# A planned attention and two-FFN kernel: twelve plan settings instead of one, another cut of d_ff, and one more engine choice

## Chip, cores and metric

The kernel runs on one core of one Trainium2 chip. The metric is the device time of one execution in microseconds; of several runs the median is given. Engines are called by their trace names where rows show them: PE is TensorE, DVE is VectorE, ACT is ScalarE, SP is SyncE, which issues the DMAs.

## The reference

Three stages follow each other. First, attention with a window and sinks (2 batches, 8 heads, 768 positions, 64 per head); then two feed-forward layers on 1536 tokens with d_model 512 and d_ff 2048, the first with a leaky activation per column (alpha), the second with softplus.

```python
keep   = (pos_k < n_sink) | ((rel >= 0) & (rel < window))   # n_sink 4, window 128
scores = where(keep, q @ k.T / sqrt(64), -1e9)
a      = exp(scores - max); a = a / (sum(a) + 1e-9); x = a @ v
h = x @ w_in1;  g = maximum(h, 0) + alpha * minimum(h, 0);       x = g @ w_out1
h = x @ w_in2;  g = maximum(h, 0) + log1p(exp(-abs(h)));         out = g @ w_out2
```

## The kernel before

Tokens are worked in four tiles (0 to 3) of 384, d_ff in 16 slices (c) of 128. An operand of a large matmul is kept as two halves: a rounded first part and the remainder (`copy`, L196, and `minus`, L205). A product is three matmuls: first by first, and the two mixed ones. For a tile and a slice, `g1` (L308) makes h with 12 matmuls into bank 4 or 5, by turns; `act1` (L328) or `act2` (L339) turns h into g and its halves on ScalarE and VectorE; `g2` (L361, layer 1) adds g's share to banks 0 to 3 with 12 matmuls; `g2_out` (L403, layer 2) does so with 9 wider ones into three banks per tile. `act2` is Abs, Exp, 1 + u (`more`, L346), Ln on the way of log1p, and three VectorE operations that put the parts together. The one at L357 is the last to read h's bank.

Weights come in eight bytes an element, and `convert` (L265) makes the two halves of one slice's weights out of them: five passes on VectorE (L291, L293, L295, L298, L206) and two on ScalarE (L282, L198). There are 16 weight buffers. Layer 2's slice c goes into the buffer of layer 1's slice c, so its load (L278) can only be issued when the last tile of layer 1 has used that slice. Attention's first loads lie in some of the same buffers.

Attention goes in 24 groups, six for each tile (`front`, L489: scores, minimum and exponential, scaling; `back`, L544: transposes, bank copies, values, halves of x).

Layer 1's order is a list of (tile, slice) at L647, made from `cuts` (L646). Tiles 0 and 1 are cut at 4 slices: tile 0 slices 0 to 3, tile 1 slices 0 to 3, tile 0 slices 4 to 15, tile 1 slices 4 to 15. Tiles 2 and 3 are cut at 8 in the same way. At the end of each run `keep_y` (L375) takes the sums out of banks 0 to 3: the first time as a copy, the second time as an add onto it (L387). For tile 3, the sum shares its memory with layer 2's step buffers of the odd slices. `split_y` (L391) makes the halves of x for layer 2 from a finished sum. Layer 2's first two tiles are cut at 8.

The order on the engines comes from a planner that runs while the program is built (`Planned`, L48). Every operation is added with a cost for each engine that may do it, the keys that it reads and writes, and a due time. `forward` (L85) is a list scheduler: at each moment a free engine takes the ready operation with the earliest due time. Where an operation may go to two engines, it is left to the other if that one would be done with it sooner, and in that comparison a queue counts: 1.8 times the cost of the ready operations on an engine that are due up to 10 us later than this one (L101 to L104). `backward` (L147) reckons from a plan how late each operation may start; `run` (L178) makes one plan from the due times written out, 12 more each from the latest starts of the one before, takes the plan with the earliest planned end, and issues the instructions in its order.

Of the kernel before, what the change touches and what calls it, by code (L numbers as in the profile page):

```python
# [34 lines left out]
class InOrder:  # L35
# [8 lines left out]
    def run(self):  # L44
        pass


class Planned:  # L48
# [33 lines left out]
            return 0.0 if a == "PE" else 0.13  # L82
        return self.AFTER[a] + (0.09 if b == "PE" else 0.0)

    def forward(self, due):  # L85

        ops = self.ops
        left = [len(o[2]) for o in ops]
        free = dict.fromkeys(self.ENGINES, 0.0)
        waiting = {e: [] for e in self.ENGINES}  # L90
        ready = {e: [] for e in self.ENGINES}
        end, on, start = {}, {}, {}

        def at(n, e):
            return max((end[b] + self.lag(on[b], e) for b in ops[n][2]), default=0.0)

        def offer(n):
            for e in ops[n][1]:
                heapq.heappush(waiting[e], (at(n, e), n))

        def queue(e, n):  # L101

            return 1.8 * sum(ops[m][1][e] for d, m in ready[e]
                             if m not in start and m != n and d <= due[n] + 10 and len(ops[m][1]) == 1)  # L104

        def elsewhere(n, e, t):
            mine = t + ops[n][1][e] + queue(e, n) - 1e-9
            return any(max(t, free[o], at(n, o)) + c + queue(o, n) < mine for o, c in ops[n][1].items() if o != e)

        for n in range(len(ops)):  # L110
            if not left[n]:
                offer(n)
        t, force = 0.0, False
        while len(start) < len(ops):
            for e in self.ENGINES:
                while waiting[e] and waiting[e][0][0] <= t + 1e-9:
                    n = heapq.heappop(waiting[e])[1]
                    if n not in start:
                        heapq.heappush(ready[e], (due[n], n))
            for e in self.ENGINES:  # L120
                if free[e] > t + 1e-9:
                    continue
                later = []
                while ready[e]:
                    d, n = heapq.heappop(ready[e])
                    if n in start:
                        continue
                    if not force and elsewhere(n, e, t):
                        later.append((d, n))
                        continue  # L130
                    start[n], end[n], on[n] = t, t + ops[n][1][e], e
                    free[e] = end[n]
                    for m in self.after[n]:
                        left[m] -= 1
                        if not left[m]:
                            offer(m)
                    break
                for x in later:
                    heapq.heappush(ready[e], x)
            nxt = [free[e] for e in self.ENGINES if free[e] > t + 1e-9]  # L140
            nxt += [waiting[e][0][0] for e in self.ENGINES if waiting[e] and waiting[e][0][0] > t + 1e-9]
            if len(start) < len(ops):
                force = not nxt
                t = min(nxt, default=t)
        return max(end.values()), start, end, on
# [32 lines left out]
    def run(self):  # L178

        self.after = [[] for _ in self.ops]  # L180
        for n, o in enumerate(self.ops):
            for b in o[2]:
                self.after[b].append(n)
        plans = [self.forward([o[3] for o in self.ops])]
        for _ in range(self.AGAIN):
            plans.append(self.forward(self.backward(*plans[-1][2:])))
        last, start, end, on = min(plans, key=lambda p: p[0])
        for n in sorted(start, key=lambda n: (start[n], n)):
            self.ops[n][0](self.nc, on[n])
# [67 lines left out]
class Ffn:  # L257
# [81 lines left out]
    def act2(self, p, due, fresh):  # L339

        add, mem, n = self.p.add, self.mem, p % 2
        h, kh = mem.bank[4 + n][:, 0:TT], ("bank", 4 + n)
        ku, kw, kl = [("step", n, i) for i in range(3)]
        (u, w, l), before = mem.step[n][0][:3], mem.step[n][1] if fresh else []

        def more(nc, e):  # L346
            if e == "ACT":
                nc.scalar.activation(w, u, AF.Copy, bias=1.0)
            else:
                nc.vector.tensor_scalar(w, u, 1.0, None, ALU.add)  # L350

        add(lambda nc, e: nc.scalar.activation(u, h, AF.Abs), {"ACT": 0.39}, [kh], [ku] + before, due)  # L352
        add(lambda nc, e: nc.scalar.activation(u, u, AF.Exp, scale=-1.0), {"ACT": 0.43}, [], [ku], due)  # L353
        add(more, {"DVE": 0.27}, [ku], [kw], due)
        add(lambda nc, e: nc.scalar.activation(l, w, AF.Ln), {"ACT": 0.43}, [kw], [kl], due)  # L355
        add(lambda nc, e: nc.vector.scalar_tensor_tensor(u, w, 1.0, u, ALU.subtract, ALU.subtract), {"DVE": 0.47}, [kw], [ku], due)  # L356
        add(lambda nc, e: nc.vector.scalar_tensor_tensor(l, h, 0.0, l, ALU.max, ALU.add), {"DVE": 0.47}, [kh], [kl], due)  # L357
        add(lambda nc, e: minus(nc, e, l, l, u), {"DVE": 0.47}, [ku], [kl], due)
        self.halves(lambda: l, kl, p, due)
# [279 lines left out]
def fast_path(tc, mem, masks, val, kqv, alpha, weights, out, loaded):  # L639


    nc = tc.nc
    plan = Planned(nc)
    ffn = Ffn(mem, plan, weights, out)
    att = Window(mem, plan, kqv)
    cuts = ((0, 4, 16), (0, 8, 16))  # L646
    layer1 = [(2 * n + t, c, a, b) for n in range(2) for a, b in zip(cuts[n], cuts[n][1:]) for t in range(2) for c in range(a, b)]  # L647
    layer2 = [(t, c) for c0 in (0, 8) for t in range(2) for c in range(c0, c0 + 8)] + [(t, c) for t in (2, 3) for c in range(16)]
    slots = 4 * [8.0] + 4 * [5.0] + 32 * [5.3] + 88 * [4.2]
    begin = [27.0]  # L650
    for s in slots:
        begin.append(begin[-1] + s)

    def at(p):

        n = max(0, min(int(p), 127))
        return begin[n] + (p - n) * slots[n]

    def groups(t):
        wanted = [8 + 3.2 * (r + 1) if t == 0 else 30 + 4 * r if t == 1 else at((0, 0, 10, 25)[t] + (0, 0.7, 2.5, 2.4)[t] * r + 0.5) for r in range(6)]  # L660
        behind = 1 if t == 1 else 0
        for r in range(6 + behind):
            if r < 6:
                G, a = 6 * t + r, wanted[r]
                if G >= loaded:
                    att.load(G, a - 20)
                att.front(G, a - 6, a - 4)
            if r >= behind:
                att.back(6 * t + r - behind, wanted[r - behind] - 2)

    plan.add(lambda nc, e: masks.first(nc, val), {"DVE": 0.9}, [("ring", 2)], [("mask", 0)], -20.0)
    for i in (1, 2):
        plan.add(lambda nc, e, i=i: masks.later(nc, i), {"DVE": 0.4}, [("ring", 2), ("mask", 0)], [("mask", i)], 5.0 * i)
    groups(0)
    groups(1)
    plan.add(lambda nc, e: nc.sync.dma_start(out=mem.alpha, in_=alpha), {"SP": 0.5}, [], [("alpha",)], 10.0)
    plan.add(lambda nc, e: nc.vector.tensor_scalar(mem.alpha, mem.alpha, -1.0, None, ALU.mult), {"DVE": 0.08}, [], [("alpha",)], 20.0)
    for c in range(16):
        d = at([p for p, x in enumerate(layer1) if x[:2] == (0, c)][0]) - 9
        ffn.convert(0, c, c, d, d - 3)  # L680
    for p, (t, c, a, b) in enumerate(layer1):
        d = at(p)
        ffn.g1(t % 3, c, p, d - 5)
        ffn.act1(c, p, d - 2)
        ffn.g2(c, p, d + 1, (c == a, c == b - 1))
        if c == b - 1:
            ffn.keep_y(t, d + 2, 4 if t == 3 and a else t, t if a else None)
        if p in (0, 23):
            groups(2 + (p == 23))
        if p == 31:  # L690
            ffn.split_y(0, 1, at(44))
        if p == 55:
            ffn.split_y(1, 2, at(58))
        if t == 3:
            w = at(42 + 2 * c if c < 8 else 64 + 2.5 * (c - 8))
            ffn.convert(1, c, c, w, w - 6)
    for p, (t, c) in enumerate(layer2):
        d = at(64 + p)
        ffn.g1((t + 1) % 3, c, p, d - 8)
        ffn.act2(p, d - 5, p < 2)  # L700
        ffn.g2_out(t, c, p, d + 1)
        if p in (0, 23):
            ffn.split_y(2 + (p == 23), p // 23, d + 10)
        if c == 15:
            ffn.store(t, d + 2)
    plan.run()
# [203 lines left out]
```

## Time and profile before

| | us |
|---|---|
| median of three runs | 636.86 (636.72 to 638.86) |
| profiled execution, its time | 637.52 |
| profiled execution, its span | 635.7 |
| PE busy | 615.2 |
| DVE busy | 478.5 |
| ACT busy | 328.9 |

The span runs from the first to the last instruction; the execution's own time is 1.8 us longer. The granted TensorE clock has a mean of 0.997 of full speed. PE's busy time is that of pipelined matmuls whose ends are modelled, so the spacing of their starts in the chain of waits is the better measure of its pace.

### The profile page before, as it was taken

The numbers are of one execution on the slowest core, as the hardware profiler recorded it, in microseconds if no ns is written. First come the engines' busy times: TensorE is split into PE (matmuls) and PEld (weight loads), VectorE is DVE, ScalarE is ACT, GpSimd is POOL, SyncE is SP. The second block draws the span as 40 slices with busy tenths as digits, with TensorE's granted clock in tenths as the row PEclk, the third lists the DMA queues.
The fourth block names the chain that finished last, engine by engine and source line by source line (L and its number), as shares of the span: only waits on it lengthen the run. The fifth ranks groups of instructions, "written<-read, shape, count | busy, mean of one in ns | idle before, by whom it ended". The sixth has DMA issues, their size and how long they took to land.

```text
span 635.7 us, 10814 instructions
## 1 busy us (share of the span) xinstructions
PE 615.2 (97%) x4192; PEld 572.1 (90%) x4192; DVE 478.5 (75%) x1119; ACT 328.9 (52%) x739; POOL 2.5 (0%) x18
## 2 busy tenths in 40 slices
PE   5789999999999999999999989999999999999996
PEld 4678999999999999999999979999999999999995
DVE  7999999955345644499966999867876777677774
ACT  4999687644533654356534765433443433343332
POOL 1000000000000000000000000000000000000000
PEclk9999999999999999999999999999999999999998
DMA  8999701121211110176007610000010100000001
GB/s 319 357 385 410 268 1 52 51 77 51 85 51 68 52 51 2 67 249 215 1 1 265 219 46 1 1 1 1 0 51 0 51 1 1 1 25 26 2 0 56
DMA packets 15035, 56.55 MB, mean 89 GB/s; under 512 B 1920, under 2 KB 4480, under 8 KB 14976
## 3 DMA queue, kind: packets, MB, share of 16 engines
q1 hardware_dynamic: 14976, 55.78, 24.5%
q8 instruction: 35, 0.57, 0.4%
q14 instruction: 24, 0.20, 0.1%
HBM read 52.63 MB, written 3.15 MB: 88 GB/s over the span
## 4 chain that ended last, share of the span: by engine, by line
PE 90%; DVE 4%; ACT 3%; issue 1%; DMA 1%; SPq 0%; ACTq 0%; DVEq 0%
PE bank L317 40%; PE bank L411 21%; PE bank L370 19%; PE bank L574 3%; PE bank L516 3%; PE bank L553 2%; PE bank L554 2%; DVE temp L298 1%; DMA temp<-kqv 1%; ACT early L527 1%; DVE g L206 0%; DVE w L206 0%; DVE r L335 0%; ACT temp L282 0%; ACT late L527 0%
## 5 line engine op out<-in xcount | busy, mean ns | idle before, releaser
L317 PE MATMUL bank<-x,w 128*128 128x384 f32 x1536 | 294.5, 337 | 2.8 <-DVE late L357 2.8
L317 PEld LDWEIGHTS bank<-x,w 128*128 128x128 f32 x1536 | 269.2, 188 | 9.7 <-DVE late L357 3.2
L370 PE MATMUL bank<-g,w 128*128 128x384 f32 x768 | 149.3, 338 | 0.0
L411 PE MATMUL bank<-w,g 128*128 128x512 f32 x576 | 143.1, 393 | 0.0
L370 PEld LDWEIGHTS bank<-g,w 128*128 128x128 f32 x768 | 133.3, 188 | 1.4
L411 PEld LDWEIGHTS bank<-w,g 128*128 128x128 f32 x576 | 107.1, 188 | 19.6
L352 ACT ACTIVATE late<-bank 128x384 f32<-128x384 f32 x64 | 31.4, 491 | 113.3 <-PE bank L317 113.3
L335 DVE SCALAR_TENSOR_TENSOR r<-r,alpha,r 128x384 f32<-128x384 f32 x64 | 39.3, 614 | 45.1 <-ACT r L334 44.8
L333 ACT ACTIVATE r<-bank 128x384 f32<-128x384 f32 x64 | 31.3, 490 | 61.7 <-PE bank L317 59.9
L350 DVE TENSOR_SCALAR late<-late 128x384 f32<-128x384 f32 x64 | 22.9, 358 | 44.0 <-ACT late L353 44.0
L355 ACT ACTIVATE late<-late 128x384 f32<-128x384 f32 x64 | 33.7, 526 | 26.1 <-DVE late L350 26.0
L527 ACT ACTIVATE late<-late,st 128x200 f32<-128x200 f32 (+1 forms) x72 | 31.8, 445 | 25.0 <-DVE st L524 25.0
L206 DVE TENSOR_TENSOR g<-late,g 128x384 fp32r<-128x384 f32 x64 | 35.6, 557 | 6.1 <-DVE g L202 0.9
L298 DVE SCALAR_TENSOR_TENSOR temp<-w,temp 128x1024 int32<-128x1024 int32 x32 | 38.8, 1215 | 1.5 <-ACT temp L282 1.5
L206 DVE TENSOR_TENSOR w<-temp,w 128x1024 fp32r<-128x1024 f32 x32 | 39.0, 1218 | 0.1
L198 ACT ACTIVATE w<-temp 128x1024 fp32r<-128x1024 f32 x32 | 34.0, 1064 | 8.1 <-DVE temp L298 8.1
L356 DVE SCALAR_TENSOR_TENSOR late<-late 128x384 f32<-128x384 f32 x64 | 35.6, 557 | 1.9
L206 DVE TENSOR_TENSOR late<-late 128x384 f32<-128x384 f32 x64 | 35.5, 557 | 1.8
L206 DVE TENSOR_TENSOR g<-r,g 128x384 fp32r<-128x384 f32 x64 | 35.5, 555 | 1.6 <-ACT g L198 0.4
L357 DVE SCALAR_TENSOR_TENSOR late<-bank,late 128x384 f32<-128x384 f32 x64 | 35.5, 556 | 0.1
L198 ACT ACTIVATE late<-bank 128x512 f32<-128x512 f32 (+2 forms) x49 | 24.8, 543 | 19.7 <-PE bank L554 14.4
L353 ACT ACTIVATE late<-late 128x384 f32<-128x384 f32 x64 | 33.6, 525 | 1.9
(98 smaller groups left out, 524.6 us busy)
## 6 DMA issues: line engine op xcount, KB each, us to landing
w<-w SPq DMA_DIRECT2D x32, 1023.8 KB, 5.8
w<-kqv SPq DMA_DIRECT2D x20, 388.0 KB, 7.3
late<-kqv SPq DMA_DIRECT2D x20, 388.0 KB, 3.5
out<-late SPq DMA_DIRECT2D x18, 128.0 KB, 1.7
spare<-kqv SPq DMA_DIRECT2D x5, 388.0 KB, 4.5
temp<-kqv SPq DMA_DIRECT2D x3, 388.0 KB, 4.4
out<-early SPq DMA_DIRECT2D x2, 256.0 KB, 3.0
out<-early SPq DMA_DIRECT2D x2, 128.0 KB, 3.9
```

Source lines behind the costliest of these rows:

```text
L198: nc.scalar.activation(out, src, AF.Copy)
L206: engine(nc, e).tensor_tensor(out, a, b, ALU.subtract)
L298: add(lambda nc, e: nc.vector.scalar_tensor_tensor(b, raw[0].rearrange("p n w -> p (n w)").bitcast(I32)[:, 0:2048:2], 13, b, ALU.logical_s ...
L317: nc.tensor.matmul(out=h, lhsT=w[:, a, kk], rhs=xt[:, b, kk], start=(kk == 0 and n == 0), stop=(kk == 3 and n == 2))
L335: add(lambda nc, e: nc.vector.scalar_tensor_tensor(n, n, mem.alpha[:, c:c + 1], r, ALU.mult, ALU.add), {"DVE": 0.54}, [("r", 0), ("alpha", ...
L353: add(lambda nc, e: nc.scalar.activation(u, u, AF.Exp, scale=-1.0), {"ACT": 0.43}, [], [ku], due)
L355: add(lambda nc, e: nc.scalar.activation(l, w, AF.Ln), {"ACT": 0.43}, [kw], [kl], due)
L356: add(lambda nc, e: nc.vector.scalar_tensor_tensor(u, w, 1.0, u, ALU.subtract, ALU.subtract), {"DVE": 0.47}, [kw], [ku], due)
L357: add(lambda nc, e: nc.vector.scalar_tensor_tensor(l, h, 0.0, l, ALU.max, ALU.add), {"DVE": 0.47}, [kh], [kl], due)
L370: nc.tensor.matmul(out=self.mem.bank[m][:, 0:TT], lhsT=w[:, a, m], rhs=g[:, b], start=(ends[0] and part == 0 and n == 0), stop=(ends[1] an ...
L411: nc.tensor.matmul(out=self.mem.bank[bk], lhsT=g[:, a, m * 128:(m + 1) * 128], rhs=w[:, b], start=(c == 0 and part == 0 and n == 0), stop= ...
L527: add(lambda nc, e, u=u: nc.scalar.activation(s[:, u, c0:], s[:, u, c0:], AF.Exp, bias=st[:, 0, u:u + 1], scale=-1.0, accum_out=st[:, 1, u ...
```

## The change

Three things are changed. `forward` takes two numbers, `ahead` and `crowd`, in place of the fixed 10 and 1.8, and `run` makes its 13 plans for each of the twelve pairs of 10, 30, 60 and 0.6, 1.0, 1.4, 1.8, then takes the plan with the earliest planned end of all. Tiles 2 and 3 are cut at 10 slices in place of 8; the halves of tile 1's result are added to the plan after tile 2's last slice, as before, which is now position 57 in place of 55. And 1 + u of `act2` may go to ScalarE, at a planner's cost of 0.43 us, beside VectorE at 0.27.

```diff
-    def forward(self, due):
+    def forward(self, due, ahead=10, crowd=1.8):
...
-            return 1.8 * sum(ops[m][1][e] for d, m in ready[e]
-                             if m not in start and m != n and d <= due[n] + 10 and len(ops[m][1]) == 1)
+            return crowd * sum(ops[m][1][e] for d, m in ready[e]
+                             if m not in start and m != n and d <= due[n] + ahead and len(ops[m][1]) == 1)
...
-        plans = [self.forward([o[3] for o in self.ops])]
-        for _ in range(self.AGAIN):
-            plans.append(self.forward(self.backward(*plans[-1][2:])))
+        plans = []
+        for ahead in (10, 30, 60):
+            for crowd in (0.6, 1.0, 1.4, 1.8):
+                plans.append(self.forward([o[3] for o in self.ops], ahead, crowd))
+                for _ in range(self.AGAIN):
+                    plans.append(self.forward(self.backward(*plans[-1][2:]), ahead, crowd))
...
-        add(more, {"DVE": 0.27}, [ku], [kw], due)
+        add(more, {"DVE": 0.27, "ACT": 0.43}, [ku], [kw], due)
...
-    cuts = ((0, 4, 16), (0, 8, 16))
+    cuts = ((0, 4, 16), (0, 10, 16))
...
-        if p == 55:
+        if t == 2 and c == 15:
             ffn.split_y(1, 2, at(58))
```

## Rows read from the trace of the kernel before

**Rows 1.** The page's busy times: engine, us busy, share, instructions.
```profile
PE 615.2 (97%) x4192; PEld 572.1 (90%) x4192; DVE 478.5 (75%) x1119; ACT 328.9 (52%) x739; POOL 2.5 (0%) x18
```

**Rows 2.** Chain of waits in order of time, full stream: start us, us, what.
```profile
326.14 2.08 PE bank L370 x12
...
332.21 2.08 PE bank L317 x12
...
548.66 2.08 PE bank L411 x9
550.74 2.10 PE bank L317 x12
```

**Rows 3.** PE's waits: line, whom it waited for, us in total, times, longest.
```profile
PE bank L516 <- DMA temp<-kqv: 5.6, 1, 5.6
PE bank L317 <- DVE late L357: 2.8, 1, 2.8
PE bank L516 <- DVE x L206: 2.1, 3, 1.1
PE bank L516 <- DVE st L531: 1.5, 1, 1.5
PE bank L574 <- ACT late L198: 1.4, 3, 0.7
PE bank L553 <- ACT early L539: 1.0, 2, 0.6
PE bank L574 <- ACT early L198: 0.5, 1, 0.5
```

**Rows 4.** Chain of waits, where the stream of PE begins.
```profile
37.64 2.02 PE bank L574 x32
39.66 2.85 PE bank L317 x15
```

**Rows 5.** Chain of waits at the change from layer 1 to layer 2.
```profile
367.64 1.14 DVE w L206
...
369.98 0.48 DVE late L357
...
370.50 2.87 PE bank L317 x15
```

**Rows 6.** Busy us by stretch; after POOL: PEclk, DMA share, GB/s.
```profile
20.00:40.00 20.00, 15.11 (x252) 11.85 (x251) 20.00 (x72) 20.00 (x63) 0.00 (x0) 1.00 0.96 364
40.00:60.00 20.00, 20.00 (x221) 17.95 (x220) 20.00 (x65) 18.73 (x51) 0.31 (x1) 1.00 1.00 400
318.00:338.00 20.00, 20.00 (x117) 20.00 (x117) 11.62 (x24) 6.18 (x14) 0.00 (x0) 1.00 0.12 41
348.00:395.00 47.00, 44.23 (x234) 41.25 (x234) 47.00 (x86) 31.88 (x54) 0.00 (x0) 1.00 0.28 99
```

**Rows 7.** Groups by line: engine, operation, shapes, count, busy us, mean ns.
```profile
L335 DVE SCALAR_TENSOR_TENSOR r<-r,alpha,r 128x384 f32<-128x384 f32 x64 | 39.3, 614 | 45.1 <-ACT r L334 44.8
L206 DVE TENSOR_TENSOR w<-temp,w 128x1024 fp32r<-128x1024 f32 x32 | 39.0, 1218 | 0.1
L298 DVE SCALAR_TENSOR_TENSOR temp<-w,temp 128x1024 int32<-128x1024 int32 x32 | 38.8, 1215 | 1.5 <-ACT temp L282 1.5
...
L353 ACT ACTIVATE late<-late 128x384 f32<-128x384 f32 x64 | 33.6, 525 | 1.9
L350 DVE TENSOR_SCALAR late<-late 128x384 f32<-128x384 f32 x64 | 22.9, 358 | 44.0 <-ACT late L353 44.0
...
L291 DVE TENSOR_SCALAR temp<-w 128x1024 bf16<-128x1024 bf16 x16 | 11.0, 689 | 0.2 <-DMA w<-w 0.2
L295 DVE TENSOR_TENSOR temp<-temp 128x1024 int16<-128x1024 int16 x16 | 11.0, 685 | 0.1
L293 DVE TENSOR_SCALAR temp<-temp 128x1024 int16<-128x1024 int16 x16 | 6.7, 420 | 0.0
```

## The prediction

> **What bounds the kernel now.** I read the page's busy times first, then TensorE's waits, then the chain of waits in order of time, and last the busy time by stretch. The busy times give TensorE 615.2 us of a 635.7 us span [rows 1]. Busy matmuls are modelled, so I checked them against the chain: in layer 2 a slice of d_ff is 12 matmuls in 2.10 us and 9 in 2.08 us, one group after the other without a gap, and in layer 1 twelve take 2.08 us [rows 2]. A slice is then 4.16 us in layer 1 and 4.18 us in layer 2, and 64 of each are 266 + 268 = 534 us. The diff leaves out or adds no matmul. So TensorE's stream can't get shorter; only its waits can. The list of them has 14.9 us in all [rows 3]: 5.6 us for the first kqv transfer, 2.8 us in one piece for VectorE's L357, and 2.1 + 1.5 + 1.4 + 1.0 + 0.5 = 6.5 us in attention. In the chain TensorE runs from 37.64 us on [rows 4], and the 2.8 us are the gap before the group that starts at 370.50 us [rows 5]. Both places are the same kind: VectorE (and at the start ScalarE too) is full and works on something less urgent. From 20 to 40 us both are busy for 20.00 of 20 us; from 348 to 395 us VectorE is busy throughout, while from 318 to 338 us it works 11.62 of 20 us [rows 6].
>
> **Tiles 2 and 3 split at 10 slices.** Layer 2's weight c goes into the buffer of layer 1's weight c, free only after tile 3 has used it. With the cut at 8, tile 3's first run frees eight buffers; tile 2 then runs eight slices in which none comes free (the lull of 318 to 338 us), and tile 3 frees the other eight in the last eight slices, when layer 2's activations begin. With the cut at 10, ten are freed early and six late. One conversion costs VectorE 689 + 420 + 685 + 1215 + 1218 ns = 4.23 us [rows 7]. Two conversions, 8.5 us of VectorE, move from the full stretch into or next to the lull, which has 20 - 11.62 = 8.4 us free; the release of the first late buffer comes two slices, 8.3 us, later. No instruction is added: both cuts make two runs of a tile, so the partial sums are kept and added as often as before.
>
> What this is worth is read at the switch. Layer 2's step buffers of the odd slices lie under tile 3's partial sum, so slice 1's Abs waits for the last add of that sum (L387). In the chain VectorE puts the last pass of a conversion (1.14 us from 367.64 us) ahead of slice 1's and 2's work, L357 has read the bank by 369.98 + 0.48 = 370.46 us, and TensorE goes on at 370.50 us [rows 5]. One such pass there and another just before it (L298 at 1215 ns [rows 7]) make up 2.4 us of the 2.8. With 8.5 us less to do by then, either can wait. A part of the series is fixed: four adds, Abs, Exp, the add, Ln, L357. I take 2.4 of 2.8 us as gone; the ends are 0 (six conversions still come at 4.23 us of VectorE for each 4.16 us slice, and the new plan may again run one there) and 2.8. Next late there is that fixed series itself, with the 0.4 us that I leave.
>
> **1 + u also on ScalarE.** Where taken, it frees 358 ns of VectorE and costs ScalarE 525 ns (Exp, the same tile and size) [rows 7]. It stands between Exp and Ln on the engine that runs both, so it delays only what follows in ScalarE's order, and spares two hand-overs. ScalarE has room in the stretch that matters: 31.88 busy of 47 us from 348 to 395 us against VectorE's 47.00 [rows 6]. In the steady part of layer 2 TensorE's 4.18 us hide either choice: no gain, no cost. At the switch, six slices moved would be 6 x 0.36 = 2.1 us of VectorE; that works on the same 2.8 us wait, so I count no second gain. If the cover is gone (ScalarE late with Abs), the loss is one extra 0.53 us a slice at the switch, at most some 1.5 us for three slices.
>
> **Twelve settings of caution instead of one.** This runs while the program is built and costs nothing on the chip. It gives 12 x 13 = 156 plans in place of 13, and the one with the earliest planned end is taken; the setting of before (10 and 1.8) is among the twelve. The planner's costs are close to what the chain has: 0.525 for three matmuls against 2.10 / 4, 1.14 for a weight's low part against the 1.14 us of rows 5, so a plan with fewer waits should have fewer on the chip. What it can win outside the switch lies before 37.64 us, since from there to the switch TensorE never waits. The 5.6 us for the first transfer stay. Of the attention waits, 1.4 + 1.0 + 0.5 = 2.9 us stand behind bank copies and scalings [rows 3], the operations with a choice of engine, which is what the settings decide; 2.1 + 1.5 = 3.6 us stand behind L206 and L531, on VectorE alone. The ends are a gain of 6.5 us and a loss of about 2.8 us (the longest wait for another engine's work in the list, once more). I take half of the 2.9 us, 1.4 us: both engines are full from 20 to 40 us, so an earlier copy makes something else late, and all that is left to gain is work put off past 37.64 us.
>
> A limit speaks against more. From 40 to 60 us the DMA engines' share is 1.00 at 400 GB/s [rows 6]: these are the weights that an earlier stream would need earlier. The Trainium skill, "Perfetto Trace Analysis", section on engine utilization (roofline), puts a single core's practical ceiling at about 435 GB/s. By it there would be 35 GB/s, some 9%, of room in that stretch, 1.6 of 20 us; by the row there is none, as the engines are already never idle. I go by the row, and it is one reason for the chance of rival 1 below.
>
> **The sum.** 2.4 + 1.4 = 3.8 us off the profiled execution's own 637.52 us (span 635.7 and 1.8 around it) is 633.7 us. That execution lies 0.66 us above the median of the runs shown, 636.86 us, so against the median the forecast is 633.0 us. What follows the last matmul is not touched.
>
> **Rivals.**
> 1. *Only the switch is won.* The new plan moves waits about in the first 40 us and gains nothing there. For it: VectorE and ScalarE at 20.00 of 20 us, DMA full behind them. Against: 2.9 us of waits behind operations that could sit on either engine. Time: 636.9 - 2.4 = 634.5 us.
> 2. *The wait at the switch only moves.* Six conversions still fall in the last six slices and the first of layer 2, the planner fills VectorE with them, and slice 1 or 2 is late by another pass of 1.2 us or two; the earlier stretch, now with ten conversions, takes what was gained. For it: VectorE is full on both sides of the switch before. Against: the lull's 8.4 us. Time: 636.9 less 0 to 1.2, say 636.3 us. That the change does next to nothing (the taken plan again cautious as before) ends here too.
> 3. *The start is much shorter.* Nearly all of the 2.9 us and half of the 3.6 us go, 4.7 in place of 1.4, for instance by conversions of slices 1 and 2 put behind attention. For it: 156 tries. Against: full engines. Time: 636.9 - 2.4 - 4.7 = 629.8 us.
> 4. *Slower: layer 1 starves in its first slices.* A bolder plan starts TensorE's stream earlier and so with fewer weights converted; each slice of tile 0 then asks VectorE for 4.23 us of conversion and about 1.6 us of activation (L335 at 614 ns, a cast taken like L350's 358 and a subtraction taken like L335's [rows 7]) against 4.16 us of TensorE, 1.7 us short a slice. Attention matmuls of the next tiles hide that now. If the stream catches up with the conversions and four slices or more aren't covered, it loses 6.8 us against the 2.4 won: 636.9 + 4.4 = 641.3 us. It decides from four slices: three cost 5.1 us, which less the 2.4 is still within 0.5%. Against it: the planner reckons with these very costs, and it did keep TensorE without a wait from 37.64 us on.
>
> **How the numbers follow.** Forecast 0.42 (own range 631.5 to 634.3), rival 1 0.22, rival 2 0.15, rival 3 0.13, rival 4 0.08. No change means within 0.5%, 633.7 to 640.0, about what a measurement of this kernel can tell. The forecast's case gives 0.37 to faster and 0.05 to no change, so faster is 0.37 + 0.13 = 0.50, same 0.05 + 0.22 + 0.15 = 0.42, slower 0.08. The range 629.5 to 637.5 us leaves out rival 4, the far half of rival 3 and the losing tail of rival 2.
>
> **What would show it.** Right: L357's 2.8 us is gone from TensorE's list or under 0.6; ten of layer 2's first passes (L291) stand before VectorE's lull and six after; the ScalarE form of 1 + u appears, most of it near the switch; the copies' waits in the first 40 us fall by about half, and the unbroken stream starts before 37.6 us by that much. Wrong: a new wait of TensorE for a weight (L206 or L198 into w) between 40 and 120 us (rival 4), an L357 or L387 wait still over 1.5 us (rival 2), or a stream that starts where it did (rival 1).

## The result, and the profile after

The changed kernel takes 632.53 us (median of five runs, 631.78 to 633.20). In the same session the kernel before took 638.66 us, so the ratio is 0.9899, with a 95% interval of 0.9876 to 0.9923: about 1% faster, or 6.1 us. The forecast of 633.0 us was made against the 636.86 us of the first three runs and a gain of 3.8 us; profile against profile the change brings 637.52 - 631.86 = 5.7 us of time, and 635.7 - 630.1 = 5.6 us of span. That span is what the steps below are set against.

The page's busy times and TensorE's list of waits after the change (line, whom it waited for, us in total, times, longest) answer to [rows 1, 3]. The lines have moved by three: L360 is the old L357, L209 the old L206.

```profile
PE 614.4 (98%) x4192; PEld 572.5 (91%) x4192; DVE 472.4 (75%) x1097; ACT 338.4 (54%) x761; POOL 2.5 (0%) x18
```

```profile
PE bank L519 <- DMA temp<-kqv: 5.6, 1, 5.6
PE bank L519 <- DVE mask L635: 1.2, 1, 1.2
PE bank L519 <- DVE x L209: 1.1, 3, 0.4
PE bank L577 <- ACT late L201: 0.8, 2, 0.6
PE bank L577 <- ACT early L201: 0.4, 1, 0.4
PE bank L320 <- DVE x L209: 0.4, 1, 0.4
PE bank L556 <- ACT early L542: 0.3, 1, 0.3
PE bank L556 <- DVE late L544: 0.2, 1, 0.2
```

Nothing waits for L360 any more. The list has 10.0 us, all of it in the first 39 us, against 14.9 before: 2.8 us went at the switch and 2.1 us at the start. The rest of the 5.6 us is a shorter stream: 0.8 us less busy time for the same 4192 matmuls. No reason for it is shown: in the other kernels of this case TensorE's busy time lies anywhere from 613.4 to 616.2 us.

The switch in TensorE's order of time, first before the change, then after (start us, us, what; idle time ahead of a row stands in brackets behind it). Layer 1's last matmuls end where the row ahead of L411 (L414) starts: at 362.90 us before and at 359.81 us after.

```profile
360.82 2.24 PE L370 MATMUL bank<-g,w 128*128 128x384 f32 x12
362.90 2.76 PE L317 MATMUL bank<-x,w 128*128 128x384 f32 x15
365.50 2.23 PE L411 MATMUL bank<-w,g 128*128 128x512 f32 x9
370.50 2.87 PE L317 MATMUL bank<-x,w 128*128 128x384 f32 x15 [2.77 <-DVE late L357]
```

```profile
359.81 3.28 PE L320 MATMUL bank<-x,w 128*128 128x384 f32 x18
362.93 2.24 PE L414 MATMUL bank<-w,g 128*128 128x512 f32 x9
365.01 2.27 PE L320 MATMUL bank<-x,w 128*128 128x384 f32 x12
```

So 3.1 us are won by the end of layer 1. Three matmuls fewer of layer 2 had been done by then, 0.5 us, which leaves 2.6 us for all that comes ahead of the switch; with the gap of 2.77 us there, that is some 5.3 of the 5.6 us.

The stretches (columns as in [rows 6]) and the two forms of 1 + u. At the start VectorE and ScalarE are as full as before, yet TensorE did 283 matmuls from 20 to 40 us where it had done 252. VectorE's lull before the switch is filled, 18.80 us for 11.62.

```profile
20.00:40.00 20.00, 17.04 (x283) 13.73 (x282) 20.00 (x77) 20.00 (x61) 0.00 (x0) 1.00 0.98 374
40.00:60.00 20.00, 20.00 (x215) 18.36 (x214) 19.71 (x62) 19.15 (x55) 0.31 (x1) 1.00 1.01 411
...
318.00:338.00 20.00, 20.00 (x118) 20.00 (x117) 18.80 (x33) 11.89 (x22) 0.00 (x0) 1.00 0.00 1
...
348.00:395.00 47.00, 47.00 (x248) 43.86 (x247) 46.50 (x84) 34.55 (x62) 0.00 (x0) 1.00 0.25 87
```

```profile
L353 DVE TENSOR_SCALAR late<-late 128x384 f32<-128x384 f32 x54 | 19.4, 360 | 45.8 <-ACT late L356 45.8
L351 ACT ACTIVATE late<-late 128x384 f32<-128x384 f32 x10 | 5.2, 521 | 0.2
```

The chain of waits where the stream begins (start us, us, what) answers to [rows 4]. TensorE's last wait ends 0.7 us later than before, at 38.37 us, but what follows it is not the same: before, it was a group of attention's values, and layer 1's first matmuls came at 39.66 us; now it is these, 1.3 us earlier, and 448 of attention's matmuls are done by then, against 424. The rows from 43.16 us on are for the last section.

```profile
37.98 0.34 DVE x L209
38.37 3.92 PE bank L320 x21
43.16 0.53 PE bank L320 x3
...
47.39 0.72 PE bank L320 x3
```

### The profile page after: what moved, and what is told of

Its sections match the earlier page's. It is cut to its first block, busy times and chain, and to the rows that moved or that the text cites. A ratio compares the mean times of both kernels' runs of the same rounds, so it can differ in the third digit from the quotient of the medians.

```text
span 630.1 us, 10818 instructions
## 1 busy us (share of the span) xinstructions
PE 614.4 (98%) x4192; PEld 572.5 (91%) x4192; DVE 472.4 (75%) x1097; ACT 338.4 (54%) x761; POOL 2.5 (0%) x18
## 4 chain that ended last, share of the span: by engine, by line
PE 95%; DVE 4%; DMA 1%; issue 0%; ACT 0%; SPq 0%
PE bank L320 43%; PE bank L373 22%; PE bank L414 21%; PE bank L519 3%; PE bank L577 3%; PE bank L556 1%; PE bank L557 1%; DMA temp<-kqv 1%; DVE late L527 1%; DVE early L527 0%; DVE temp L301 0%; DVE x L205 0%; DVE x L209 0%; DVE late L205 0%; DVE temp L294 0%
## 5 line engine op out<-in xcount | busy, mean ns | idle before, releaser
L320 PE MATMUL bank<-x,w 128*128 128x384 f32 x1536 | 295.6, 337 | 0.4 <-DVE x L209 0.4
L320 PEld LDWEIGHTS bank<-x,w 128*128 128x128 f32 x1536 | 269.3, 188 | 7.3 <-DVE x L209 0.5
L414 PE MATMUL bank<-w,g 128*128 128x512 f32 x576 | 143.1, 393 | 0.0
L414 PEld LDWEIGHTS bank<-w,g 128*128 128x128 f32 x576 | 107.2, 188 | 19.6
L353 DVE TENSOR_SCALAR late<-late 128x384 f32<-128x384 f32 x54 | 19.4, 360 | 45.8 <-ACT late L356 45.8
L209 DVE TENSOR_TENSOR g<-late,g 128x384 fp32r<-128x384 f32 x64 | 35.7, 557 | 5.8 <-DVE g L205 0.5
L209 DVE TENSOR_TENSOR w<-temp,w 128x1024 fp32r<-128x1024 f32 x32 | 38.8, 1215 | 0.0
L209 DVE TENSOR_TENSOR late<-late 128x384 f32<-128x384 f32 x64 | 35.6, 557 | 1.9
L209 DVE TENSOR_TENSOR g<-r,g 128x384 fp32r<-128x384 f32 x64 | 35.4, 553 | 1.7 <-ACT g L201 0.6
L360 DVE SCALAR_TENSOR_TENSOR late<-bank,late 128x384 f32<-128x384 f32 x64 | 35.6, 556 | 0.1
```

The costliest lines, as they stand in the source:

```text
L209: engine(nc, e).tensor_tensor(out, a, b, ALU.subtract)
L320: nc.tensor.matmul(out=h, lhsT=w[:, a, kk], rhs=xt[:, b, kk], start=(kk == 0 and n == 0), stop=(kk == 3 and n == 2))
L414: nc.tensor.matmul(out=self.mem.bank[bk], lhsT=g[:, a, m * 128:(m + 1) * 128], rhs=w[:, b], start=(c == 0 and part == 0 and n == 0), stop= ...
```

## The experiments

Twelve more kernels were run: the three parts alone and in pairs, two orders of VectorE's work at the switch, 1 + u put back, and three kernels with work left out at the start. In the table, *start* is the sum of TensorE's waits up to the switch, *switch* the sum there, both in us from each run's list of waits. Each ratio is to the kernel before in the same session, where it had medians of 638.3 to 638.9 us.

| kernel | median us | ratio to before (95%) | span | start | switch |
|---|---|---|---|---|---|
| before | | | 635.7 | 12.1 | 2.8 |
| cut | 635.52 | 0.9955 (0.9935 to 0.9975) | 633.3 | 11.5 | 0.5 |
| act | 636.57 | 0.9971 (0.9955 to 0.9987) | 634.7 | 11.6 | 1.4 |
| plans | 634.00 | 0.9938 (0.9919 to 0.9956) | 631.7 | 9.3 | 0.8 |
| cut_act | 634.78 | 0.9945 (0.9925 to 0.9965) | 632.6 | 11.8 | 0 |
| cut_plans | 633.43 | 0.9925 (0.9895 to 0.9954) | 630.6 | 10.6 | 0.6 |
| act_plans | 633.52 | 0.9926 (0.9899 to 0.9954) | 630.9 | 10.0 | 0.9 |
| all three | 632.53 | 0.9899 (0.9876 to 0.9923) | 630.1 | 10.0 | 0 |
| more_back | 632.96 | 0.9911 (0.9885 to 0.9937) | 630.5 | 10.2 | 0 |
| two_passes_later | 639.11 | 1.0016 (1.0002 to 1.0030) | 636.3 | 11.9 | 3.5 |
| three_passes_later | 638.27 | 0.9994 (0.9982 to 1.0006) | 636.7 | 11.7 | 3.3 |
| three_less_dve | 631.89 | 0.9889 (0.9871 to 0.9908) | 630.2 | 9.1 | 0 |
| three_less_act | 632.04 | 0.9888 (0.9869 to 0.9906) | 630.5 | 9.8 | 0 |
| three_less_both | 630.74 | 0.9886 (0.9861 to 0.9911) | 629.3 | 9.4 | 0 |

One of the start's waits, 0.4 to 1.5 us ahead of the scores at 10 us, comes and goes between kernels of one and the same planned start, and is put down to a mask, a statistic or a transfer (w<-kqv) by turns; a difference of half a us in that column says nothing. Without that wait the start is 10.6 us in the kernel before, cut, act and cut_act, and 8.7 to 8.8 us in plans, act_plans, more_back and the changed kernel: the settings are worth 1.8 to 1.9 us of waits there.

**The cut alone.**

```diff
-    cuts = ((0, 4, 16), (0, 8, 16))
+    cuts = ((0, 4, 16), (0, 10, 16))
-        if p == 55:
+        if t == 2 and c == 15:
```

> The cut of tiles 2 and 3 at 10 slices alone, with the 13 plans of before and 1 + u on VectorE only. Theory A (two separate gains: the cut relieves VectorE at the switch of layers, the settings shorten the first 40 us): TensorE's wait for L357 falls from 2.8 us to under 0.6, its waits in the first 40 us stay at 12 us, and the time falls by 2.4 to 2.8 us, ratio 0.996. Rival B (the choice among 156 plans wins both, and the cut only gives the planner another problem): L357's wait stays above 1.5 us and the time moves by less than 1 us.

As theory A had it: the span falls by 2.4 us, and the wait at the switch from 2.8 to 0.5.

```profile
PE bank L317 <- DVE late L357: 0.5, 1, 0.5
```

**The twelve settings alone.**

```diff
-        plans = [self.forward([o[3] for o in self.ops])]
...
+        for ahead in (10, 30, 60):
+            for crowd in (0.6, 1.0, 1.4, 1.8):
+                plans.append(self.forward([o[3] for o in self.ops], ahead, crowd))
```

> The twelve settings alone, tiles 2 and 3 still cut at 8, 1 + u on VectorE only. Theory A: the waits of the first 40 us fall from 12.1 to about 10 us, the L357 wait at the switch stays over 1.5 us, the time falls by about 2.6 us, ratio 0.996. Rival B: the L357 wait goes too and the time falls by 5 us or more, ratio 0.992 or less.

4.0 us of span and a ratio of 0.9938, between the two theories. The start falls to 9.3 us, and the wait at the switch, with the cut still at 8, to 0.8.

```profile
PE bank L519 <- DVE x L209: 1.1, 3, 0.4
PE bank L320 <- DVE late L360: 0.8, 1, 0.8
PE bank L577 <- ACT late L201: 0.7, 2, 0.6
```

So the settings win at both places, and the cut isn't needed for most of the switch. Theory A was wrong in giving each part a place of its own.

**1 + u alone.**

```diff
-        add(more, {"DVE": 0.27}, [ku], [kw], due)
+        add(more, {"DVE": 0.27, "ACT": 0.43}, [ku], [kw], due)
```

> 1 + u also on ScalarE alone, cut at 8, 13 plans. The prediction counted no gain of its own for it beside the cut; alone it takes up to 0.36 us of VectorE per slice off the switch. Theory A: L357's wait falls by 0.4 to 1.5 us, the start is as before, ratio 0.998 to 0.999. Rival C (ScalarE's copy in the way of Abs at the switch costs as much as it frees): no change, L357's wait at 2.8 us or more.

1.0 us of span; L357's wait is 1.1 us, a little less than theory A had left of it, and 0.3 us came up behind the halves of g. Rival C falls.

```profile
PE bank L317 <- DVE late L357: 1.1, 1, 1.1
...
PE bank L411 <- DVE g L206: 0.3, 1, 0.3
```

**The pairs.** Each is the changed kernel with one part undone.

```diff
cut_act:    -        for ahead in (10, 30, 60):   (and the rest of the settings)
cut_plans:  -        add(more, {"DVE": 0.27, "ACT": 0.43}, [ku], [kw], due)
            +        add(more, {"DVE": 0.27}, [ku], [kw], due)
act_plans:  -    cuts = ((0, 4, 16), (0, 10, 16))
            +    cuts = ((0, 4, 16), (0, 8, 16))
```

> The changed kernel without the twelve settings: cut at 10, 1 + u also on ScalarE, 13 plans. Theory A (the start belongs to the settings, the wait at the switch is taken away by either of cut and settings, so the parts overlap there): the waits of the first 40 us are 11 to 12 us again, L357 waits at most 0.5 us, ratio 0.994 to 0.996, as with the cut alone. Rival C (1 + u on ScalarE has a gain of its own of some 2 us, as the run with it alone suggests): ratio 0.992 or less.

> The changed kernel with 1 + u on VectorE only: cut at 10 and twelve settings. Theory A: no wait at the switch over 0.5 us, waits at the start as in the changed kernel, ratio 0.990 to 0.991, the changed kernel's own within its interval. Rival C: about 2 us lost against it, ratio 0.993.

> The changed kernel with tiles 2 and 3 cut at 8 again: twelve settings, 1 + u also on ScalarE. Theory A: the settings alone left 0.8 us of wait for L357; with ScalarE's help 0 to 0.8 us is left, ratio 0.991 to 0.993. If the cut is still needed beside the settings, as the prediction had it, L357 waits over 1.5 us and the ratio is 0.994 or more.

cut_act came as theory A had it. cut_plans did not quite: 0.6 us of wait are left at the switch where A asked for 0.5 at most, and 0.9925 is nearer to rival C's 0.993, with an interval that covers both. act_plans keeps 0.9 us, just over A's 0.8, and far from the 1.5 us at which the cut would still have been needed. The settings undone cost 2.5 us of span, and the start's waits are back; the cut undone 0.8; 1 + u undone 0.5. The parts alone add up to 2.4 + 1.0 + 4.0 = 7.4 us and together give 5.6: they share the 2.8 us of the switch. Between cut_plans, act_plans and the changed kernel the intervals overlap. That the last us needs all three is what the medians and spans suggest, and isn't shown beyond doubt.

**1 + u put back on VectorE in the changed kernel's own order.**

```diff
         last, start, end, on = min(plans, key=lambda p: p[0])
+        on = {n: "DVE" if self.ops[n][0].__name__ == "more" else e for n, e in on.items()}
```

> The changed kernel's own order of instructions, but the ten 1 + u that it gives to ScalarE are done by VectorE, in the same places. Theory A (no gain of its own): less than 0.5 us slower, no wait of TensorE over 0.5 us at the switch. Rival C: slices 0, 1 and 2 of layer 2 are each late by VectorE's 0.36 us, L357 waits 1 us or more, 1 to 2 us slower than the changed kernel.

0.4 us by median and by span, with intervals that overlap, and no wait at the switch: theory A.

**Two, then three conversion passes later at the switch.** The kernel before, with its own plan, and only the places of these passes changed. The numbers are the planner's: 1890 is the L298 and 1892 the subtraction of slice 12, with ScalarE's copy, 1891, between them; 1867 is the subtraction of slice 11; 2008 is slice 1's L357, 2030 the last half of g of slices 1 and 2, and 2042 and 2043 are slice 3's Exp and 1 + u.

```diff
         last, start, end, on = min(plans, key=lambda p: p[0])
+        read = start[2008]
+        start[1867], start[1890], start[1891] = read + 0.475, read + 0.48, read + 0.49
```

> The kernel before with its own order, except that two conversion passes of VectorE just ahead of the stall at the switch (L298 of slice 12, L302's subtraction of slice 11) and the ScalarE pass that follows the first are issued right after slice 1's L357. The prediction's step: these two passes make up 2.4 us of the 2.8 us stall, so the stall falls to about 0.4 us and the time by 2.3 us. Rival D (the stall is mostly the fixed series: slice 1's Abs starts at 366.1 us, and Exp, 1 + u, Ln and L357 follow it): the stall falls by about 1.2 us only, to 1.6 us.

L357's wait fell to 1.3 us, as rival D had it, but 2.2 us came back behind a copy of g on ScalarE. The chain shows why: that copy stood behind the weights' copy, which now waited for the pass on VectorE.

```profile
370.61 1.15 DVE temp L300
...
371.78 1.06 ACT w L200
372.83 0.83 ACT g L200 x2
...
373.71 2.34 PE bank L413 x9
```

The next order therefore puts all passes behind the halves of g.

```diff
         last, start, end, on = min(plans, key=lambda p: p[0])
+        start[1867], start[1890] = start[2030] + 0.26, start[2030] + 0.27
+        start[1891], start[1892] = start[2042] + 0.75, start[2043] + 0.35
```

> The kernel before with its own order, except that three conversion passes of VectorE at the switch are issued after the halves of slices 1 and 2 of layer 2, and the ScalarE pass between them after the copies of these halves, so that ScalarE's order isn't held up (as it was in the run with two passes moved, where 2.2 us of wait came back behind a copy of g). Theory D (the stall of 2.8 us is about 1.5 us of conversion passes and 1.3 us of the fixed series from slice 1's Abs to its L357): L357's wait is 1.3 us again, no wait for a copy of g over 0.5 us, time 1.0 to 1.5 us under the kernel before, ratio 0.998. The prediction's step (2.4 us are conversion passes): wait 0.4 us, 2.3 us faster, ratio 0.9963.

Neither theory. The first wait is 1.3 us, as D says, and no copy holds TensorE up, but two of the next readings of the bank are late in their turn (TensorE's matmuls in order of time, idle time in brackets):

```profile
369.17 2.90 PE L319 MATMUL bank<-x,w 128*128 128x384 f32 x15 [1.26 <-DVE late L359]
...
378.95 2.35 PE L319 MATMUL bank<-x,w 128*128 128x384 f32 x12 [1.12 <-DVE late L359]
...
384.29 2.38 PE L319 MATMUL bank<-x,w 128*128 128x384 f32 x12 [0.91 <-DVE late L359]
```

The stall was no matter of one pass in a bad place. Once put off, the passes make L357 late two and three slices later, among activations that leave VectorE no room. This is rival 2 of the prediction, which did not come with the cut at 10 but does come where only the order is changed.

**Less work at the start.** The changed kernel's own order, with passes left out in the conversion of layer 1's slices 0 to 2: VectorE's, ScalarE's, then both.

```diff
three_less_dve, three_less_both:
-        add(lambda nc, e: nc.vector.scalar_tensor_tensor(
+        add(lambda nc, e: None if l == 0 and c < 3 else nc.vector.scalar_tensor_tensor(
three_less_act, three_less_both:
-        add(place, {"ACT": 0.96}, [kz], [kv], due)
+        add((lambda nc, e: None) if l == 0 and c < 3 else place, {"ACT": 0.96}, [kz], [kv], due)
```

> The changed kernel's own order, with VectorE's pass L301 (1.14 us each) left out in the conversion of layer 1's slices 0 to 2, so that these weights are not what they should be. What binds the first 38 us? Theory E (VectorE's work, of which the new plan puts some off): the stream of TensorE starts 2 to 3.4 us earlier and the time falls by 2 us or more against the changed kernel. Rival F (ScalarE is as full and binds): less than 0.7 us. Rival G (transfers: DMA engines full from 20 to 60 us): no change, and a wait for w<-kqv or for weights comes up.

> The changed kernel's own order, with ScalarE's pass L285 (0.95 us each) left out in the conversion of layer 1's slices 0 to 2, so that these weights are not what they should be. Theory E (VectorE binds the start): less than 0.7 us faster than the changed kernel. Rival F (ScalarE binds): the stream starts 1.5 to 2.8 us earlier and the time falls by as much.

Neither gains: spans of 630.2 and 630.5 us against 630.1. The medians, 631.89 and 632.04 us, are from another session than the changed kernel's 632.53, and the ratios' intervals overlap. The stretch of 20 to 40 us, first with VectorE relieved, then with ScalarE relieved, shows that the relieved engine does get free time and the matmuls stay at 284:

```profile
20.00:40.00 20.00, 17.12 (x284) 13.71 (x283) 18.15 (x76) 20.00 (x61) 0.00 (x0) 1.00 0.99 362
```

```profile
20.00:40.00 20.00, 16.62 (x284) 13.76 (x283) 20.00 (x78) 18.65 (x60) 0.00 (x0) 1.00 0.98 372
```

Theories E and F fall, each as told. Of rival G the half came true that nothing changes; no new wait for a weight came up.

> The changed kernel's own order, with both passes left out in the conversion of layer 1's slices 0 to 2 (VectorE's L301 and ScalarE's L285), so that these weights are not what they should be. Each alone gave nothing: the chain went over to the other engine. Theory H (the two engines bind the start together, by turns): with both relieved the stream of TensorE starts 2 to 3 us earlier and the time falls by 1.5 us or more against the changed kernel. Rival G (neither binds; the order of attention's own steps and transfers fixes when x of tile 0 is complete): the stream starts within 0.5 us of 38.4 us, and no more than 0.5 us is gained.

The stream starts at 37.76 us, 0.6 us earlier, and 0.8 us of span are gained. The wait at 10 us blurs this; from the scores behind it to the stream, the changed kernel and the two with one engine relieved take 20.1 us, and this one 19.1 us. First the changed kernel, then the one with both passes left out:

```profile
18.26 0.92 PE L519 MATMUL bank<-w 64*64 64x200 f32 x24 [0.43 <-DVE x L209]
...
38.37 3.92 PE L320 MATMUL bank<-x,w 128*128 128x384 f32 x21 [0.36 <-DVE x L209]
```

```profile
18.65 0.92 PE L519 MATMUL bank<-w 64*64 64x200 f32 x24 [0.43 <-DVE x L209]
...
37.76 3.91 PE L320 MATMUL bank<-x,w 128*128 128x384 f32 x21 [0.36 <-DVE x L209]
```

So 1.0 us is won, where theory H asked for 2 to 3 us and G for 0.5 at most; neither is right, and the runs' times, whose intervals overlap the changed kernel's, can't decide. In the changed kernel only two of the three passes of each kind stand ahead of 37.6 us, 2.4 us of VectorE and 2.1 us of ScalarE. Relieving one engine wins nothing and relieving both wins less than half of what was taken away, so the two together do bind the start, but only a part of it. That the rest lies in attention's own steps, each behind the one before on another engine, is argued and not shown. How much an order planned for the lighter work would win wasn't tried.

## Why the prediction was right, and where it wasn't

*The time.* 633.0 against 632.53 us, and faster as forecast. Both places where time was to be won are the places where most of it was won: 2.8 us at the switch, and at the start 1.8 us of waits besides the one at 10 us. The gain was undersized, 3.8 against 5.6 us of span, in both its terms. That the forecast still lies within 0.5 us of the median is luck: the kernel before had a median of 638.66 us in the session of the result, 1.8 us above the one that the forecast started from, and the two misses nearly cancel.

*The switch: 2.4 us forecast, 2.8 us measured.* The size for the cut is right by the run with the cut alone (2.8 to 0.5 us), but as it was worked out that is luck. Two things behind it were wrong. The step said that two conversion passes in a bad place make up 2.4 of the 2.8 us, and that "either can wait". Moved, they gained nothing; what has to go is work out of the full stretch, which the cut does by bringing two conversions forward into the lull, and that part of the step held: with the cut alone VectorE is busy for 20.00 us from 318 to 338 us, and for 21.55 of 23 us from 348 to 371 us against 23.00 before. And the settings, which the prediction put at the start alone, take 2.0 of the 2.8 us by themselves with the cut at 8. In that run ScalarE is busy for more of the switch (17.74 of 23 us from 348 to 371 us against 16.56 before) and VectorE just as full; that a better share-out between the two is the reason is likely but was not tested.

*1 + u: no second gain forecast.* Right within the noise: put back in the same order it costs 0.4 us, left out of the planning 0.5 us of span, and ten of 64 slices used it, eight of them between 357 and 390 us. Alone it takes 1.4 us off the wait at the switch, the same wait as the others.

*The start: 1.4 us forecast, 2.1 us of waits measured, some 2.6 us by the end of layer 1.* The term of the sum that was mis-sized. The waits behind copies and scalings fell from 2.9 to 0.8 + 0.4 + 0.3 + 0.2 = 1.7 us, 1.2 of the expected 1.4. The other 0.9 us came from waits that the prediction left as they were because they hang on VectorE alone: L206 from 2.1 to 1.1 + 0.4 us, and the 1.5 us to 1.2, which is the wait at 10 us that comes and goes. The reason given, that work put off past the stream's start is all there is to win, is in part what the new plan did: the last two passes of one conversion no longer stand ahead of 37.6 us, about 1.1 us of ScalarE and 1.2 us of VectorE (groups by line from 0 to 37.6 us, before, then after).

```profile
L206 DVE TENSOR_TENSOR w<-temp,w 128x1024 fp32r<-128x1024 f32 x2 | 2.4, 1209 | 0.0
L198 ACT ACTIVATE w<-temp 128x1024 fp32r<-128x1024 f32 x2 | 2.1, 1060 | 0.0
```

```profile
L209 DVE TENSOR_TENSOR w<-temp,w 128x1024 fp32r<-128x1024 f32 x1 | 1.2, 1210 | 0.0
L201 ACT ACTIVATE w<-temp 128x1024 fp32r<-128x1024 f32 x1 | 1.1, 1060 | 0.0
```

How much of the gain comes from that is not shown; four more passes left out moved the stream by 1.0 us. The prediction's sign for it, an unbroken stream that starts before 37.6 us, failed: it starts at 38.37 us, and the gain is in what is done by then. The other part is another order of attention's steps; which of the planner's decisions make it stays open.

*A conversion's cost.* 4.23 us adds up profiled durations. Back to back in the full stretch, the passes stand 0.60 + 0.34 + 0.60 + 1.13 + 1.14 = 3.81 us apart in the chain of the kernel before, less than a slice's 4.16. The sum doesn't use the figure, but the lower end of the switch and rival 4 were drawn too dark by it.

*The rivals.* Rival 1 (a start that gains nothing) would have left 12.1 us of waits there; 10.0 are left. Rival 2 is away in the changed kernel: of layer 2's conversions, the first pass, L294, starts ten times up to 318.2 us and six times from 343.17 us on, as the cut should make it. Rival 3 (4.7 us at the start) asked for about twice what came. Rival 4 did not come: after 39 us TensorE waits for no weight.

*The DMA limit.* The prediction read a share of 1.00 at 400 GB/s as no room. The changed kernel moved 411 GB/s in the same 20 us, and the kernel with 1 + u alone, with the start of before, did so too: some room was there. The Trainium skill's ceiling of about 435 GB/s ("Perfetto Trace Analysis", section on engine utilization) was not reached in that stretch by any run; 417 GB/s is the most. In the changed kernel's list TensorE waits for a transfer only at 5.6 us, the first one.

## What to carry to other kernels

When an engine is full through a stretch, moving its less urgent work a little later may only move the wait, as it did here; look for a stretch where it idles and for what keeps the work out of it, here a buffer freed too late. Gains of parts that relieve the same wait don't add: run them alone and in pairs before giving each a share. And an engine that is busy for 20 of 20 us need not be what sets the time; leaving out some of its work shows it at the cost of one run, and where two engines are full, leave out work of each alone and of both.

## What was not expected of the hardware

The first full-array group behind attention's 64-wide matmuls takes longer. In the chain of the changed kernel three L320 matmuls take 0.53 us behind transposes (at 43.16 us) and 0.72 us behind the values of attention (at 47.39 us): 0.19 us more. The Trainium skill says that changing the tiling mode drains the engine ("TensorEngine Tiling (Array Packing)", key properties); the rows agree, and 0.19 us is the price here. That the drain is what costs it was not tested by itself. TensorE's order of time has 35 such places in this kernel, 20 behind values and 15 behind scores, so by an estimate some 6.7 us of the span; the kernel before also has 35, but 21 of them behind values, and ten changes from scores or values to transposes, against eight. The kernel with the settings alone has the same 20, 15 and eight as the changed kernel, and its TensorE is busy for 615.6 us, more than before the change; so these places don't explain the 0.8 us of busy time that went. An order with fewer changes was not tried.

The share of the DMA engines is no fixed rate: 1.00 went with 400 GB/s before the change, and with both passes left out at the start the same stretch shows

```profile
40.00:60.00 20.00, 20.00 (x218) 18.11 (x218) 18.69 (x60) 18.73 (x53) 0.31 (x1) 1.00 1.01 417
```
